# A hand-ordered attention, mixture and softplus-MLP kernel on one core: the first load of w_in moved behind the last expert matrices, and the order of everything after it written anew

## The chip, the cores and the metric

The kernel runs on one NeuronCore of a Trainium2 chip; the other seven cores are idle. The metric is device time in microseconds (us) of one execution. Five engines work side by side, each through its own instructions in program order: TensorE (PE in the profile; its weight loads are the row PEld), VectorE (DVE), ScalarE (ACT), GpSimd (POOL) and SyncE (SP), which here only issues DMA transfers. An engine that meets an instruction whose inputs are not there waits, and everything behind it on that engine waits too.

## What is computed

Three layers follow one another. The change lies behind the first.

```
x = block attention of q, k, v                        # 1536 tokens x 512
# a soft mixture of 8 experts with 4 slots each
logits = x @ phi
slot_input = softmax over tokens(logits).T @ x        # 32 x 512
for e in range(8):
    slot_out[e] = maximum(slot_input[e] @ w1[e], 0) @ w2[e]
x = softmax over slots(logits) @ slot_out             # 1536 x 512
# a softplus MLP
h = x @ w_in                                          # 512 x 2048
out = (maximum(h, 0) + log1p(exp(-abs(h)))) @ w_out   # 2048 x 512
```

## The kernel before

Everything is written as small named tasks. The string ORDER_A lists the tasks of the attention, ORDER_B those of the experts and the MLP; `run` (L188) issues them in the order of the list, and so the list alone sets the order of instructions on every engine. An engine's own order is the list with the other engines' tasks struck out. The change is a new ORDER_B; ORDER_A and all functions stay.

**Experts.** The 32 slots are one small matrix, so the time goes into loading 8 x 4 MB of weights. All transfers go through SP's one queue, 1 MB each: `w2 e h` is half h of the second matrix of expert e, `wi c h` a piece of w_in (tile wi_raw, L239), `wo b h` a piece of w_out (tile wo_raw, L249). On PE, `hu` makes the hidden rows of two experts (L751), `ht` turns them (L762), `dn e h` multiplies a half of an expert's second matrix and adds it to one sum in PSUM (so_ps, L773, four products of 512 columns), `yl n` does the last half of expert 7 in two pieces of 256 columns (L784). One source matmul of these stands as two in the trace.

**From the experts to the MLP.** `so` copies the sum out of PSUM on ACT, `ya n` adds the pieces of `yl` on DVE (L788), `yt n` turns the result on PE (L794), and `ye n` puts it into soT: the 32 slot outputs, transposed. The MLP never forms the 1536 x 512 mixture. It multiplies soT with w_in first (2048 columns in 8 parts p), as `swc 0` (L865) for part 0 and `swa p` (L850), `swb p`, `swc p` (L862) for the others; `swd p` and `swe p` put a rounded copy and its rest into cs ("SW").

**Unpacking.** w_in and w_out arrive as 64-bit numbers and are turned into 32-bit ones by hand, part by part: `wia p` or `woa p` on ACT (L680), then `wib p 0..2` or `wob p 0..2` on DVE (L686, L688, L691). `wh p` on ACT and `wl p` on DVE split a part of w_out into a high and a low half (tile whl).

**The MLP.** Half R = 0 or 1 of the tokens and column block J make step n = 16 R + J. `ha n` makes h on PE (f_ps, L881; the two banks exist once), `hx n` is the softplus on ACT (L889, tile e), `hh n` its rounded high half on ACT (gh), `hl n` the rest on DVE (gl, L732). Then 18 products of 512 columns add to six sums (acc, L907): `m n p h` are three of them, with p = 0 and 1 reading gh and p = 2 reading gl; p = 1 reads the low half of w_out, and in the first and last step of a half `m n t` does the three products of one sum. At the end of a half, `leave R t` copies a sum out (ACT or DVE) and `out R t` sends it. `swa p` and `swc p` write into spare columns of the f_ps tile of a step n, so they wait until `hx n` has read it.

```
def sw_a(p):
    ...
    o = parts["a", p] = f[2 * p - 2][:, 0, 384:512]
...
def hid(n):
    ...
    f[n] = ps_f.tile([128, 2, 512], F32, tag="f", name="f_ps")
```

The order around the change, in the list: `w2 6 1, hu 2 1, hu 3 0, wi 0 0, w2 7 0, w2 7 1`, and later `dn 5 1, yl 0, dn 6 0, dn 6 1, woa 0, dn 7 0, wob 0 0, wob 0 1, yl 1, so`.

Of the kernel before, what the change touches and what calls it, by code (L numbers as in the profile page):

```python
# [23 lines left out]
wo 1 1, wi 2 1, ya 0, wo 2 0, ct 2, ya 1, yt 0, cc 1, wob 0 2, ye 0:ACT, cc 2, yt 1, wib 1 0, wh 0, ye 1:DVE, swc 0,
wib 1 1, wia 2, wl 0:DVE, swd 0:ACT, woa 1, swe 0, wib 1 2, ha 0, fp, hx 0 0, hh 0 0, swa 1, hx 0 1, wib 2 0, wi 3 0,
wo 2 1, wi 3 1, hh 0 1, hl 0 0, m 0 0, swb 1:ACT, wia 3, hl 0 1, m 0 1, wib 2 1, ha 1, m 0 2, hx 1, wib 2 2, m 0 3,
hh 1, wob 1 0, m 0 4, woa 2, hl 1, m 0 5, swc 1, wob 1 1, m 1 0 0, swd 1:ACT, wia 4, swe 1, m 1 0 1, wob 1 2, ha 2,
m 1 1 1, hx 2, wib 3 0, wo 3 0, wo 3 1, m 1 2 1, wh 1, wib 3 1, m 1 1 0, hh 2, m 1 2 0, wl 1:DVE, m 2 0 0, hl 2,
m 2 1 0, woa 3, swa 2, wib 3 2, wia 5, m 2 2 0, swb 2:ACT, wob 2 0, ha 3, wob 2 1, m 2 0 1, hx 3, m 2 1 1, hh 3,
wob 2 2, m 2 2 1, swc 2, hl 3, wh 2, m 3 0 1, swd 2:DVE, wia 6, m 3 1 1, wl 2:DVE, m 3 2 1, swe 2, woa 4, m 3 0 0,  # L30
wib 4 0, ha 4, wib 4 1, m 3 1 0, hx 4, m 3 2 0, hh 4, wib 4 2, swa 3, hl 4, m 4 0 1, swb 3:ACT, wia 7, wob 3 0, ha 5,
m 4 1 1, hx 5, wob 3 1, m 4 2 1, hh 5, m 4 0 0, wob 3 2, m 4 1 0, hl 5, wh 3, m 4 2 0, m 5 0 0, wib 5 0, wl 3:DVE,
m 5 1 0, m 5 2 0, wib 5 1, woa 5, swc 3, m 5 0 1, swd 3:ACT, wib 5 2, m 5 1 1, swe 3, m 5 2 1, wob 4 0, ha 6,
wob 4 1, hx 6, swa 4, hh 6, wob 4 2, m 6 0 1, swb 4:ACT, hl 6, wh 4, m 6 1 1, ha 7, wib 6 0, m 6 0 0, hx 7, wl 4:DVE,
m 6 1 0, hh 7, m 6 2 0, wib 6 1, woa 6, m 6 2 1, hl 7, swc 4, m 7 0 1, swd 4:ACT, wib 6 2, m 7 1 1, swe 4, m 7 2 1,
wob 5 0, ha 8, wob 5 1, m 7 0 0, hx 8, m 7 1 0, hh 8, wob 5 2, m 7 2 0, m 8 0 0, hl 8, wh 5, m 8 1 0, wib 7 0,
m 8 2 0, wl 5:DVE, m 8 0 1, m 8 1 1, wib 7 1, woa 7, m 8 2 1, wib 7 2, swa 5, swb 5:ACT, wob 6 0, ha 9, wob 6 1,
hx 9, swc 5, hh 9, wob 6 2, m 9 0 1, swd 5:ACT, hl 9, m 9 0 0, wh 6, m 9 1 1, swe 5, wl 6:DVE, ha 10, m 9 1 0, hx 10,
m 9 2 0, wob 7 0, hh 10, wob 7 1, m 9 2 1, m 10 0 0, hl 10, m 10 1 0, wob 7 2, m 10 0 1, m 10 2 0, wh 7, swa 6,
m 10 1 1, wl 7:DVE, swb 6:ACT, ha 11, m 10 2 1, hx 11, swc 6, hh 11, swd 6:DVE, m 11 0 0, hl 11, m 11 1 0, swe 6,  # L40
m 11 2 0, ha 12, m 11 0 1, hx 12, m 11 1 1, hh 12, m 11 2 1, hl 12, m 12 0 1, m 12 0 0, m 12 1 0, m 12 2 0, m 12 1 1,
swa 7, m 12 2 1, swb 7:ACT, ha 13, hx 13, swc 7, hh 13, swd 7:DVE, m 13 0 1, hl 13, m 13 0 0, swe 7, m 13 1 0,
m 13 2 0, ha 14, m 13 1 1, hx 14, m 13 2 1, hh 14, ha 15, hl 14, m 14 0 0, hx 15, m 14 1 0, hh 15, m 14 2 0, hl 15,
m 14 0 1, m 14 1 1, m 14 2 1, m 15 4, m 15 0, ha 16, leave 0 0:ACT, m 15 3, hx 16, out 0 0, m 15 1, hh 16, m 15 5,
leave 0 1:ACT, hl 16, ha 17, out 0 1, m 15 2, hx 17, m 16 0, hh 17, leave 0 2:DVE, m 16 1, leave 0 3:ACT,
leave 0 4:DVE, out 0 2, leave 0 5:ACT, m 16 2, hl 17, out 0 3, out 0 4, out 0 5, m 16 3, m 16 4, m 16 5, ha 18,
m 17 0 1, hx 18, m 17 1 1, hh 18, m 17 2 1, hl 18, m 17 0 0, m 17 1 0, m 17 2 0, ha 19, m 18 0 0, hx 19, m 18 1 0,
hh 19, m 18 2 0, hl 19, m 19 0 0, m 19 1 0, m 18 0 1, m 18 1 1, m 18 2 1, m 19 0 1, m 19 1 1, ha 20, m 19 2 0, hx 20,
m 19 2 1, hh 20, ha 21, hl 20, m 20 0 0, hx 21, m 20 1 0, hh 21, m 20 0 1, hl 21, m 20 1 1, m 20 2 1, m 20 2 0,
m 21 0 0, m 21 0 1, m 21 1 1, m 21 2 1, ha 22, m 21 1 0, hx 22, m 21 2 0, hh 22, ha 23, hl 22, m 22 0 0, hx 23,  # L50
m 22 1 0, hh 23, m 22 2 0, hl 23, m 22 0 1, m 22 1 1, m 22 2 1, m 23 0 0, m 23 0 1, m 23 1 1, m 23 2 1, ha 24,
m 23 1 0, hx 24, m 23 2 0, hh 24, ha 25, hl 24, m 24 0 1, hx 25, m 24 0 0, hh 25, m 24 1 0, hl 25, m 24 2 0,
m 24 1 1, m 24 2 1, ha 26, m 25 0 0, hx 26, m 25 1 0, hh 26, m 25 2 0, hl 26, m 25 0 1, m 25 1 1, m 25 2 1, m 26 0 0,
m 26 1 0, ha 27, m 26 0 1, hx 27, m 26 1 1, hh 27, m 26 2 1, hl 27, m 26 2 0, ha 28, m 27 0 1, hx 28, m 27 1 1,
hh 28, m 27 2 1, hl 28, m 27 0 0, m 27 1 0, m 27 2 0, m 28 0 1, ha 29, m 28 0 0, hx 29, m 28 1 0, hh 29, m 28 2 0,
hl 29, m 28 1 1, m 28 2 1, m 29 0 1, ha 30, m 29 0 0, hx 30, m 29 1 0, hh 30, m 29 2 0, hl 30, m 29 1 1, m 29 2 1,
ha 31, m 30 0 1, hx 31, m 30 1 1, hh 31, m 30 2 1, hl 31, m 30 0 0, m 30 1 0, m 30 2 0, m 31 4, m 31 1, m 31 3,
m 31 0, m 31 5, leave 1 0:ACT, leave 1 1:DVE, out 1 1, m 31 2, out 1 0, leave 1 2:ACT, leave 1 3:DVE, leave 1 4:DVE,
# [917 lines left out]
```

## Time and profile before

| | |
|---|---|
| median of 3 runs | 317.62 us (316.42 to 318.15) |
| profiled execution | 317.56 us, its span 315.3 us, mean granted TensorE clock 0.977 |
| PE busy | 288.4 us (91% of the span) |
| DVE busy | 160.0 us (51%) |
| ACT busy | 131.1 us (42%) |
| DMA | 66.87 MB, mean 212 GB/s |
| chain that ended last, by engine | PE 61%, DVE 15%, DMA 12%, ACT 6% |
| largest line of that chain | PE acc L907, 36% |

The span runs from the first to the last instruction; 2.26 us of the execution lie around it. PE's 91% is an average over stages. The chain of waits goes back from the last instruction and names at each step what released it; its shares tell which engine the end waited for. A granted clock of 1.0 is TensorE's 2.4 GHz, 0.5 its 1.2 GHz.

### The profile page before, as it was taken

What the parts mean: (1) busy time and instruction counts of PE and PEld (TensorE: products, weight loads), DVE (VectorE), ACT (ScalarE), POOL (GpSimd) and SP (SyncE); (2) the same over time, 40 slices, a digit from 0 to 9 for tenths busy, and PEclk for the clock granted to TensorE, in tenths of its full rate; (3) what the DMA queues carried; (4) which work ended last, traced back from release to release, by engine and by line L of the source; (5) the groups of instructions that cost most, each with busy time, mean ns of one, the idle gap of its engine ahead of it and who ended that gap; (6) DMA issues with size and microseconds to landing.
All of it is one profiled execution on the core that took longest, in us unless ns stands there. A gap on an engine that the chain in (4) does not pass through costs nothing.

```text
span 315.3 us, 5651 instructions
## 1 busy us (share of the span) xinstructions
PE 288.4 (91%) x2385; PEld 196.6 (62%) x2385; DVE 160.0 (51%) x243; ACT 131.1 (42%) x197; POOL 33.5 (11%) x78
## 2 busy tenths in 40 slices
...
GB/s 237 408 421 405 420 404 418 419 418 382 273 397 70 409 424 409 403 395 400 393 401 168 0 0 3 0 0 2 0 33 166 2 0 0 0 2 0 0 0 200
DMA packets 17464, 66.87 MB, mean 212 GB/s; under 512 B 1952, under 2 KB 2080, under 8 KB 13344
## 3 DMA queue, kind: packets, MB, share of 16 engines
...
q14 instruction: 6, 0.05, 0.0%
...
## 4 chain that ended last, share of the span: by engine, by line
PE 61%; DVE 15%; DMA 12%; ACT 6%; issue 3%; SPq 1%; POOL 0%; DVEq 0%; ACTq 0%
PE acc L907 36%; DMA s<-in_moe_w 9%; PE f_ps L881 3%; PE av L365 3%; DMA s<-in_v 3%; PE tpa L349 2%; PE vs_ps L282 2%; PE sc L327 2%; DVE wf L688 2%; PE h_ps L751 2%; PE tpx L387 2%; PE so_ps L773 2%; DVE AB L339 1%; DVE m L332 1%; DVE wf L691 1%
## 5 line engine op out<-in xcount | busy, mean ns | idle before, releaser
L907 PE MATMUL acc<-whl,gh 128*128 128x512 f32 x384 | 106.6, 405 | 1.6 <-ACT gh L180 1.4
L907 PEld LDWEIGHTS acc<-whl,gh 128*128 128x128 f32 x384 | 71.5, 190 | 19.8 <-ACT gh L180 4.2
L732 DVE TENSOR_TENSOR gl<-e,gh 128x768 fp32r<-128x768 f32 (+1 forms) x33 | 30.7, 931 | 66.3 <-ACT gh L180 46.5
L907 PE MATMUL acc<-whl,gl 128*128 128x512 f32 x192 | 57.2, 396 | 0.0
L889 ACT ACTIVATE e<-f_ps 128x768 f32<-128x768 f32 (+1 forms) x33 | 26.2, 792 | 59.6 <-PE f_ps L881 58.9
L907 PEld LDWEIGHTS acc<-whl,gl 128*128 128x128 f32 x192 | 35.8, 188 | 9.1 <-issue 0.4
L180 ACT ACTIVATE gh<-e 128x768 fp32r<-128x768 f32 (+1 forms) x33 | 27.3, 826 | 1.1
L344 ACT ACTIVATE AB<-AB 128x480 f32<-128x480 f32 x24 | 13.2, 598 | 17.6 <-DVE AB L339 17.4
L881 PE MATMUL f_ps<-cs 128*128 128x384 f32 x64 | 17.0, 347 | 2.2 <-DVE cs L732 1.8
L332 DVE TENSOR_REDUCE m<-sc 128x8 f32<-128x960 f32 x12 | 13.8, 1154 | 8.8 <-PE sc L327 8.7
L349 PE MATMUL tpa<-ident,AB 128*120 128x128 f32 x96 | 14.4, 284 | 1.8 <-ACT AB L344 0.6
L881 PEld LDWEIGHTS f_ps<-cs 128*128 128x128 f32 x64 | 11.7, 190 | 6.5 <-DVE cs L732 2.8
L751 PE MATMUL h_ps<-s,siT 128*32 128x512 f32 x128 | 15.6, 648 | 0.1
L365 PE MATMUL av<-s,AB 120*64 120x65 f32 x384 | 14.0, 225 | 1.7 <-ACT AB L180 1.1
L365 PEld LDWEIGHTS av<-s,AB 120*64 120x64 f32 x384 | 12.3, 137 | 4.5 <-POOL s L258 2.2
L773 PE MATMUL so_ps<-s,hT 128*32 128x512 f32 x104 | 14.6, 697 | 0.0
L339 DVE TENSOR_TENSOR AB<-sc,m 128x960 f32<-128x960 f32 x12 | 13.9, 1155 | 1.4 <-PE tpa L349 0.7
L180 ACT ACTIVATE AB<-tpa 120x512 f32<-120x512 f32 x23 | 13.1, 593 | 3.1 <-PE tpa L349 3.0
L618 PE MATMUL wm<-warm_x 128*128 128x480 bf16 x43 | 13.1, 449 | 1.2 <-DVE warm_x L599 1.2
...
L349 PEld LDWEIGHTS tpa<-ident,AB 128*120 128x120 f32 x96 | 10.0, 137 | 6.2 <-ACT AB L344 1.8
L680 ACT ACTIVATE wo<-wo_raw 128x1024 f32<-128x1024 f32 x8 | 9.2, 1147 | 10.8 <-DMA wo_raw<-in_moe_w_out 6.3
(130 smaller groups left out, 311.1 us busy)
## 6 DMA issues: line engine op xcount, KB each, us to landing
...
```

What stands on the lines that cost most here:

```text
L180: nc.scalar.activation(out=o, in_=i, func=ACTF.Copy)
L332: nc.vector.tensor_reduce(out=m.rearrange("p (e u) -> p e u", e=2), in_=sc_t[i][:, :, 0:480].rearrange("p e (u j) -> p e u j", u=4), axis= ...
L339: nc.vector.tensor_tensor(out=A_t[i], in0=sc_t[i][:, :, 0:480].rearrange("p e (u j) -> p e u j", u=4), in1=m_t[i].rearrange("p (e u) -> p ...
L344: nc.scalar.activation(out=A_t[i][:, e], in_=A_t[i][:, e], func=ACTF.Exp, scale=0.125)
L349: nc.tensor.transpose(tp[0:120, u], A_t[i][:, e, u, :], ident)
L365: mm(out=av_t[i][64 * w:64 * w + 64, e, 65 * u:65 * u + 65], lhsT=AT_t[i][0:120, e, c:c + 64], rhs=v_t[g][0:120, 4 * n + 2 * t + w, 2 * a ...
L732: (nc.vector if eng == "DVE" else nc.gpsimd).tensor_tensor(out=o, in0=i, in1=h.bitcast(F32), op=ALU.subtract)
L751: mm(out=h_ps[E][32 * j:32 * j + 32], lhsT=siT[:, kk], rhs=w1_t[2 * E + j // 2, n][:, kk % 2, 512 * (j % 2):512 * (j % 2) + 512], start=(k ...
L773: mm(out=so_ps[32 * m:32 * m + 32, 0], lhsT=hT[e // 4][:, e % 4, h, m], rhs=w2_t[e, h, m], start=(e == 0 and h == 0), stop=(e == 7 and h = ...
L881: mm(out=f[n][:, h, 0:384], lhsT=cs_t["SW"][:, J], rhs=cs_t["cS"][:, s0:s0 + 384], **one)
L889: nc.scalar.activation(out=e_[n][:, half(hs)], in_=f[n][:, half(hs), 0:384], func=ACTF.Softplus)
L907: mm(out=acc[R, t], lhsT=g, rhs=(wh, wl, wh)[p][J], start=(J == 0 and p == 0), stop=(J == 15 and p == 2))
```

## The change

The string ORDER_B is replaced by another order of the same tasks. Seven tasks change their engine: `swd 2` and `swd 6` go from DVE to ACT, and five of the twelve copies `leave` at the ends of the halves are dealt out anew. Of the diff two lines say what leads it:

```
-w2 5 1, w2 6 0, hu 2 0, w2 6 1, hu 2 1, hu 3 0, wi 0 0, w2 7 0, w2 7 1, hu 3 1, ht 0, wo 0 0, wi 0 1, wi 1 0, wo 0 1,
+w2 5 1, w2 6 0, hu 2 0, w2 6 1, w2 7 0, hu 2 1, w2 7 1, hu 3 0, wi 0 0, hu 3 1, ht 0, wo 0 0, wi 0 1, wi 1 0, wo 0 1,
...
+wia 0, dn 5 1, wib 0 0, dn 6 0, wib 0 1, dn 6 1, woa 0, wib 0 2, dn 7 0, wob 0 0, wob 0 1, yl 0, so, yl 1, wia 1,
```

**Place 1, SP and PE at the last experts.** SP's queue before, from the last w2 loads on:

```order
L231 DMA s<-in_moe_w 128x2048 x8
L239 DMA wi_raw<-in_moe_w_in 128x4x512
L231 DMA s<-in_moe_w 128x2048 x2
L249 DMA wo_raw<-in_moe_w_out 128x2x1024
L239 DMA wi_raw<-in_moe_w_in 128x4x512 x2
```

and of the change:

```order
L231 DMA s<-in_moe_w 128x2048 x10
L239 DMA wi_raw<-in_moe_w_in 128x4x512
L249 DMA wo_raw<-in_moe_w_out 128x2x1024
L239 DMA wi_raw<-in_moe_w_in 128x4x512 x2
```

The first piece of w_in stood ahead of both halves of expert 7 and now stands behind them; from wo_raw on the queue is as it was. PE before, from the experts 4 to 7 (hT_1407) to the first part of w_in:

```order
L773 MATMUL so_ps<-s,hT_1407 32x512 x16
L784 MATMUL so_ps<-s,hT_1407 32x256 x4
L773 MATMUL so_ps<-s,hT_1407 32x512 x12
L784 MATMUL so_ps<-s,hT_1407 32x256 x4
L670 MATMUL ct_ps<-ident,cw 128x128 x8
L794 MATMUL sT_ps<-e_99,so 128x128 x4
L865 MATMUL sw_ps<-wf,soT 128x128 x8
```

and of the change:

```order
L773 MATMUL so_ps<-s,hT_1407 32x512 x28
L784 MATMUL so_ps<-s,hT_1407 32x256 x8
L670 MATMUL ct_ps<-ident,cw 128x128 x4
L794 MATMUL sT_ps<-e_99,so 128x128 x4
L865 MATMUL sw_ps<-wf,soT 128x128 x8
```

`yl 0` stood ahead of the last three `dn` (x12) and now stands with `yl 1` behind them; one `ct` went forward. On DVE the order from the first `wib` to `swe 0` is the same in both: `wib 0 0..2`, `wob 0 0`, `wob 0 1`, then `ya`; on ACT `so` stands behind `woa 0` in both.

**Place 2, PE in the steps 3 to 5 (f_ps L881 is `ha`, L850 `swa 3`, L862 `swc 3`).** Of the change:

```order
L907 MATMUL acc<-whl,gl 128x512 x3
L881 MATMUL f_ps<-cs 128x384 x2
L850 MATMUL f_ps<-wf,soT 32x128 x8
L907 MATMUL acc<-whl,gh 128x512 x3
L881 MATMUL f_ps<-cs 128x384 x2
L907 MATMUL acc<-whl,gh 128x512 x3
```

`ha 4` and `swa 3` had six products of step 3 between them and now stand side by side. The same pair side by side was there before at `ha 6`, `swa 4`, and is there now at `ha 4`, `ha 6` and `ha 8`; the pair `ha`, `swc` was side by side before at `ha 9` and `ha 13`.

**Place 3, PE between the two halves of the tokens (the sums of step 15 in threes: two of gh, one of gl).** Before:

```order
L907 MATMUL acc<-whl,gl 128x512
L881 MATMUL f_ps<-cs 128x384 x2
L907 MATMUL acc<-whl,gh 128x512 x2
L907 MATMUL acc<-whl,gl 128x512
L907 MATMUL acc<-whl,gh 128x512 x2
L907 MATMUL acc<-whl,gl 128x512
L907 MATMUL acc<-whl,gh 128x512 x2
L907 MATMUL acc<-whl,gl 128x512
L881 MATMUL f_ps<-cs 128x384 x2
L907 MATMUL acc<-whl,gh 128x512 x2
```

and of the change:

```order
L907 MATMUL acc<-whl,gh 128x512 x2
L907 MATMUL acc<-whl,gl 128x512
L907 MATMUL acc<-whl,gh 128x512 x2
L907 MATMUL acc<-whl,gl 128x512
L881 MATMUL f_ps<-cs 128x384 x4
L907 MATMUL acc<-whl,gh 128x512 x2
L907 MATMUL acc<-whl,gl 128x512
```

`ha 16` stood after two of the six sums of step 15 and `ha 17` after five; now both stand behind all six, next to each other (x4), and ahead of the first sum of step 16. On ACT the copies `leave 0 0`, `leave 0 2` and `leave 0 3` stand ahead of `hx 16`. At the very end the last sum is in both orders `m 31 2`; behind its copy on ACT, `leave 1 2`, the list now has one more copy on ACT, `leave 1 5`, which was on DVE.

## Rows read from the trace of the kernel before

**Rows 1.** Chain that ended last: start, us, what (the last expert loads, the products behind)

```profile
110.83 20.19 DMA s<-in_moe_w
132.23 5.00 PE so_ps L773 x24
```

**Rows 2.** Timeline 120 to 138 us: start, us, engine, line, tile, count [idle before <-releaser]

```profile
121.95 3.64 PE L773 MATMUL so_ps<-s,hT 128*32 128x512 f32 x32
131.15 1.08 PE L784 MATMUL so_ps<-s,hT 128*32 128x256 f32 x8 [5.56 <-DMA s<-in_moe_w]
...
126.25 1.12 ACT L680 ACTIVATE wf<-wi_raw 128x1024 f32<-128x1024 f32 x1 [6.92 <-DMA wi_raw<-in_moe_w_in]
133.62 1.14 ACT L680 ACTIVATE wo<-wo_raw 128x1024 f32<-128x1024 f32 x1 [6.26 <-DMA wo_raw<-in_moe_w_out]
137.32 0.60 ACT L180 ACTIVATE so<-so_ps 128x512 f32<-128x512 f32 x1 [2.55 <-PE so_ps L773]
...
129.39 1.22 DVE L691 SCALAR_TENSOR_TENSOR wf<-wi_raw,wf 128x1024 int32<-128x1024 int32 x1
...
137.95 0.42 DVE L788 TENSOR_TENSOR so<-so_ps,so 128x256 f32<-128x256 f32 x1 [1.19 <-ACT so L180]
```

**Rows 3.** Timeline 138 to 146 us, the way into the MLP

```profile
138.49 0.65 PE L794 MATMUL sT_ps<-e,so 128*128 128x128 f32 x4
...
140.34 2.35 PE L865 MATMUL sw_ps<-wf,soT 128*128 128x128 f32 x16
...
143.33 0.43 DVE L732 TENSOR_TENSOR cs<-sw_ps,cs 64x256 fp32r<-64x256 f32 x1
...
145.74 0.73 PE L907 MATMUL acc<-whl,gh 128*128 128x512 f32 x2
```

**Rows 4.** Stages: from:to, us, busy PE, PEld, DVE, ACT, POOL, granted clock, DMA

```profile
131.10:137.60 6.50, 6.45 (x41) 1.99 (x41) 1.92 (x2) 1.43 (x2) 0.00 (x0) 0.55 1.04 390
...
160.00:178.00 18.00, 17.77 (x93) 13.27 (x92) 17.64 (x20) 11.95 (x14) 0.00 (x0) 1.00 0.51 197
```

**Rows 5.** Timeline 178 to 223 us: steps 6, 9 and 13 on PE, step 6 on ACT

```profile
178.01 0.62 PE L881 MATMUL f_ps<-cs 128*128 128x384 f32 x2 [0.25 <-DVE cs L732]
178.66 0.81 ACT L889 ACTIVATE e<-f_ps 128x768 f32<-128x768 f32 x1 [2.09 <-PE f_ps L881]
179.51 0.85 ACT L180 ACTIVATE gh<-e 128x768 fp32r<-128x768 f32 x1
...
179.53 0.64 PE L850 MATMUL f_ps<-wf,soT 128*32 128x128 f32 x16 [0.90 <-ACT e L889]
...
180.41 0.50 PE L907 MATMUL acc<-whl,gh 128*128 128x512 f32 x1 [0.23 <-ACT gh L180]
...
198.00 3.91 PE L907 MATMUL acc<-whl,gh 128*128 128x512 f32 x9 [0.38 <-ACT gh L180]
...
222.69 2.37 PE L907 MATMUL acc<-whl,gh 128*128 128x512 f32 x9 [0.38 <-ACT gh L180]
```

**Rows 6.** A stretch of one us at step 9, columns as rows 4

```profile
199.00:200.00 1.00, 1.00 (x3) 0.76 (x3) 0.97 (x2) 0.87 (x1) 0.00 (x0) 0.50 0.00 0
```

**Rows 7.** Chain that ended last: one `ha`, `swc`, `swa`, and 36 products

```profile
182.07 0.35 PE f_ps L881 x2
...
185.23 0.42 PE f_ps L862 x4
...
207.17 0.57 PE f_ps L850 x16
...
301.94 8.42 PE acc L907 x36
```

**Rows 8.** The page's costliest groups: busy us, mean ns of one | idle before

```profile
L732 DVE TENSOR_TENSOR gl<-e,gh 128x768 fp32r<-128x768 f32 (+1 forms) x33 | 30.7, 931 | 66.3 <-ACT gh L180 46.5
```

**Rows 9.** Timeline, the last product and the last copy

```profile
309.94 0.40 PE L907 MATMUL acc<-whl,gl 128*128 128x512 f32 x1
...
310.38 0.60 ACT L180 ACTIVATE ot<-acc 128x512 f32<-128x512 f32 x1 [0.80 <-PE acc L907]
```

More of the change, by code (lines that the diff above doesn't have):

```diff
@@ L24 @@
[L24 to L58, printed above, removed]
@@ L59 @@
-out 1 3, leave 1 5:DVE, out 1 4, out 1 5, out 1 2
+hu 0 0, c 0, w2 3 0, hu 0 1, w2 3 1, w2 4 0, hu 1 0, hr 0, w2 4 1, c 1, c 2, w2 5 0, hu 1 1, c 3, c 5, c 4, c 6,
+w2 5 1, w2 6 0, hu 2 0, w2 6 1, w2 7 0, hu 2 1, w2 7 1, hu 3 0, wi 0 0, hu 3 1, ht 0, wo 0 0, wi 0 1, wi 1 0, wo 0 1,
+wi 1 1, ct 0, hr 2, hc 0 0, dn 0 0, hc 0 1, cc 0, dn 0 1, dn 1 0, dn 1 1, ht 2, hr 1, hc 2 1, hc 2 0, ht 1, ct 1,
+hc 1 1, hr 3, hc 1 0, dn 2 0, cc 1, dn 2 1, ht 3, dn 3 0, hc 3 1, hc 3 0, dn 3 1, dn 4 0, wo 1 0, dn 4 1, dn 5 0,
@@ new lines @@
+wia 0, dn 5 1, wib 0 0, dn 6 0, wib 0 1, dn 6 1, woa 0, wib 0 2, dn 7 0, wob 0 0, wob 0 1, yl 0, so, yl 1, wia 1,
+ya 0, ct 2, wi 2 0, ya 1, wo 1 1, wi 2 1, wo 2 0, yt 0, wob 0 2, cc 2, ye 0:ACT, yt 1, wib 1 0, wh 0, ye 1:DVE,
+swc 0, wib 1 1, wia 2, wl 0:DVE, swd 0:ACT, woa 1, swe 0, wib 1 2, ha 0, fp, hx 0 0, hh 0 0, swa 1, hx 0 1, wib 2 0,
+wi 3 0, wo 2 1, wi 3 1, hh 0 1, hl 0 0, m 0 0, wia 3, hl 0 1, m 0 1, wib 2 1, swb 1:ACT, m 0 2, wib 2 2, ha 1, m 0 3,
+woa 2, wob 1 0, m 0 4, hx 1, wob 1 1, m 0 5, hh 1, swc 1, hl 1, m 1 0 0, wia 4, wob 1 2, m 1 1 0, swd 1:ACT, m 1 0 1,
@@ new lines @@
+swe 1, wh 1, wo 3 0, wo 3 1, m 1 1 1, wib 3 0, m 1 2 1, wib 3 1, ha 2, m 1 2 0, wl 1:DVE, hx 2, swa 2, hh 2, wib 3 2,
+m 2 0 1, woa 3, m 2 0 0, wob 2 0, swb 2:ACT, wia 5, hl 2, ha 3, m 2 1 1, hx 3, wob 2 1, m 2 2 1, hh 3, m 2 1 0, hl 3,
+m 2 2 0, wob 2 2, m 3 0 0, wia 6, m 3 0 1, wib 4 0, wh 2, swc 2, wib 4 1, m 3 1 1, swd 2:ACT, m 3 2 1, wl 2:DVE,
+m 3 1 0, swe 2, woa 4, m 3 2 0, wib 4 2, ha 4, hx 4, wob 3 0, swa 3, hh 4, wob 3 1, m 4 0 1, swb 3:ACT, wia 7, hl 4,
+ha 5, m 4 1 1, hx 5, wob 3 2, m 4 2 1, hh 5, wib 5 0, swc 3, wh 3, m 4 0 0, hl 5, swd 3:ACT, m 4 1 0, swe 3,
```

31 lines of the change are left out of this document (27 added, 4 removed).

## The prediction

> **What bounds the kernel now.** I read the chain of waits first, because it shows what the end waited for. Up to 131 us it is the loading of the expert matrices: the last link of it is one DMA piece of 20.19 us, and then 24 products on PE [rows 1]. The timeline of that place [rows 2] shows why these products are slow and late. PE was done with expert 5 at 125.59 (121.95 + 3.64). The next instruction in its queue was `yl 0`, which needs the very last load; it waited 5.56 us, and with it the products of expert 6 and of the first half of 7, whose data lay there. Then the 24 products took 5.00 us, 0.21 each, where 32 of the same kind had taken 3.64, 0.114 each: the granted clock from 131.1 to 137.6 has a mean of 0.55 [rows 4], that is mostly 1.2 GHz after an idle stretch, and 2.4 GHz before it. `so` began on ACT at 137.32, and DVE waited 1.19 us for it.
>
> From `ya` at 137.95 on, DVE and ACT share the chain with PE until about 200 us. In the stage from 160 to 178 us PE is busy 17.77 us of 18 and DVE 17.64 [rows 4]: neither has room, and a delay of one is a delay of both. From 223 us to the end PE alone counts: 36 products take 8.42 us [rows 7] back to back. So the question is how much idle PE time goes ahead of 146 us, and how much the new order puts in or takes out behind it. The sum is made against the profiled execution, 317.56 us (span 315.3 and 2.26 around it), which is the median of the runs within 0.1 us.
>
> **A. The experts' end, -0.45 us.** The loads land one behind another: ACT got w_in's first piece at 126.25, PE the last expert half at 131.15 two loads later, ACT w_out's first at 133.62 [rows 2], so about 2.45 us each. In the new queue the two expert halves land at about 126.2 and 128.7 and w_in's piece at 131.15; w_out's stays. PE then does its 24 products as the data come, at 2.4 GHz, and both `yl` by about 130: the 5.56 us wait and the half-speed products are gone from there. But little of it reaches `ya`. `so` stands on ACT behind `woa 0`, whose load lands at 133.62, so it begins at 134.8. And `ya` stands on DVE behind five field operations. The first three cannot begin before 131.15 + 1.12 = 132.3, and take 3.24 us (126.25 + 1.12 to 129.39 + 1.22 [rows 2]): 135.5. The two of w_out take the same less the third field, 3.24 - 1.22 = 2.0: 137.5. `ya` was at 137.95. Bounds: nothing gained, and -1.2, DVE's whole wait.
>
> **B. The clock on the way into the MLP, +2.0.** What is late next is PE itself. It now idles from about 130 to 137.5, longer than the 5.56 us after which it ran at 1.2 GHz, and so begins the critical part there: `yt`, `swc 0`, `ha 0`. Before, the slow stretch fell on the 24 products and was over at 137. The two groups of `yt` take 0.65 each at most and the `swc 0` 2.35 with a wait of about 0.2 to 0.7 in it [rows 3]; at the ratio 0.21/0.114 = 1.85 they take some 2.8 us more. Some 0.8 of that fits into waits that are there now. `swe 0`, at 143.33 before, and the first product of `m 0 0`, at 145.74, come 2.0 later by this term. Bounds: 0, the clock being back by then; and +3.8, if the first products of step 0 are slow too (one slow stretch cost 1.8, see C).
>
> **C. Steps 0 to 12, -1.7.** From the first product to step 13 the trace has 222.69 - 145.74 = 76.95 us. The work in it is 13 x 18 products at 0.234 (8.42/36), 54.7; 13 `ha` at 0.35, 4.6; 6 `swa` at 0.57, 3.4; 7 `swc` at 0.42, 2.9 [rows 7]: 65.6. So 11.3 are lost. A round trip is seen at step 6 [rows 5]: `swa 4` starts 1.52 after `ha 6`, the next product 2.40 after it. A pair `ha`, `swa` side by side thus costs 1.52 - 0.35 = 1.17, then 2.40 - 1.52 - 0.57 = 0.31: 1.5. A pair `ha`, `swc` costs 1.6. Before, the order forces 5.7: the pair at step 6, pairs with `swc` at 9 (with a further 0.4 for the copy ahead of it) and 13, and 0.6 where three products stand between, at 11. At step 9 the clock also fell: 0.50 at 199 us [rows 6], nine products in 3.91 instead of 2.1 [rows 5], 1.8 lost. The new order forces 6.2: pairs at 4, 6 and 8, 4.5, and 1.7 at 2 and 13, where three products stand between. Waits of this length did not drop the clock at step 6, so I take the 1.8 as saved: 6.2 - 5.7 - 1.8 = -1.3. `swd 2` leaves the full DVE, about -0.4, the size of `swe` [rows 3]. Bounds: -3.6, if half of what is left of the 11.3 (3.8, waits for DVE and changes of tile) goes as well; and +0.1, if one of the new pairs drops the clock.
>
> **D. Between the halves, +2.3.** Before, `ha 16` lay under the sums of step 15 and cost nothing. Now it is behind all of them. Count from the end of the last one, 0: the copy `leave 0 3` starts on ACT 0.2 later (310.38 against 309.94 + 0.234 [rows 9]) and ends at 0.8; `hx 16` runs to 1.6, `hh 16` to 2.45 [rows 5], `hl 16` on DVE 0.93 more, about 3.45 with the handing over [rows 8]. PE does `ha 16` to 0.35, waits for `hx 16`, does `ha 17` from 1.65 to 2.0, starts `m 16 0` at 2.5, and its third product, which needs gl, waits from 2.97 to 3.5. Lost: 1.3 + 0.5 + 0.5. Bounds: 1.6, if ACT is early; and 4.1 if the clock falls there as at step 9.
>
> **E. Later steps, +1.5.** The new list has `ha 21, m 20 2 1, hx 21, hh 21, ha 22, hx 22, m 21 0 1`: three products and `ha 22` under a round trip of 1.52 and 2.40, so 0.47 and 0.52 are lost. `m 31 0` needs gl of step 31, 2.40 + 0.93 = 3.33 after `ha 31`; PE is there at 0.35 + 3 x 0.70 + 0.47 = 2.9: 0.5. **F. The end, +0.6.** One more copy on ACT, 0.60 [rows 9], stands behind the last one, and its transfer goes out last.
>
> **Sum:** -0.45 + 2.0 - 1.7 + 2.3 + 1.5 + 0.6 = +4.25, from 317.56 to **321.8 us**. What is moved past SP's queue costs nothing: the DMA share is 1.04 at 131 to 137 us [rows 4], so the transfers wait for each other and not for SP.
>
> **Rivals.** *The clock is never low behind the experts* (B is 0): for it speaks that `yt` could fall into a stretch that the chip still grants; against it the idle time, longer than one that did lower it. 317.56 + 2.25 = 319.8, and within 0.5% (1.6 us, about what a measurement of this kernel can tell from no change) if C goes a little further. *The clock falls again*, at a pair or between the halves: +1.8 to +3.6, 323.6 to 325.4; for it speaks step 9, against it step 6. *The other side: PE no longer waits for DVE between 146 and 223 us.* In place of 11.3 only the forced 6.2 would be lost, C is -5.1; with the clock up at `yt` that makes -0.45 - 5.1 + 4.4 = -1.15, 316.4, or a little below. It decides at `ha 4` and `ha 10`: if `swe 2` and `swe 5` are done before PE gets there, this holds. Against it: DVE is busy 17.64 of 18 us and does the same fields as before. [...]
>
> **Chances.** Forecast 0.52; clock never low 0.15, of which 0.09 within 0.5%; clock falling again 0.15; other side 0.13, of which 0.08 faster by over 0.5%; landings unchanged 0.05. So faster 0.08, same 0.09 + 0.05 = 0.14, slower 0.78. The range leaves out the other side, part of the clock rival and the worst of the bounds: 318.3 to 325.5.
>
> **What would show it.** In the profile of the change PE should idle from about 130 to 137.5, the clock be 0.5 behind it, `ya` start near 137.5, `m 0 0` near 147.3, PE wait about 1.2 between `ha` and `swa` at steps 4, 6 and 8, and 2.3 in all at the change of halves. If `m 0 0` starts before 146, B is wrong; if PE is dense between the halves, D; if step 13 starts 5 us earlier counted from `m 0 0`, the other side holds.

## The result and the profile after

The changed kernel takes 320.88 us, median of 16 executions (317.6 to 324.69), beside 316.47 of the kernel before (16 executions, 314.09 to 318.35): ratio 1.0116, 95% interval 1.0086 to 1.0145, so 3.7 us slower (2.7 to 4.6). The ratio leaves out executions that lie over 1.5% above the fastest of their kernel, three of the 16 of the change, so it is below the 1.0139 of the two medians. The profiled execution took 321.95 us, its span 320.2, mean granted clock 0.963 (before 0.977); it is 4.39 longer than the profiled one of before.

The loads landed as their new order says: both halves of expert 7 (`yl` at 128.51), then w_in's first piece (its copy at 130.74), then w_out's (133.18). Timeline of the change, 124 to 152 us, PE, then ACT and DVE (start, us, engine, line, tile, count [idle before <-releaser]):

```profile
123.79 4.90 PE L773 MATMUL so_ps<-s,hT 128*32 128x512 f32 x44
128.51 1.05 PE L784 MATMUL so_ps<-s,hT 128*32 128x256 f32 x16
...
137.36 1.22 PE L794 MATMUL sT_ps<-e,so 128*128 128x128 f32 x4 [7.22 <-DVE so L788]
139.05 1.22 PE L794 MATMUL sT_ps<-e,so 128*128 128x128 f32 x4 [0.47 <-ACT soT L180]
140.06 3.48 PE L865 MATMUL sw_ps<-wf,soT 128*128 128x128 f32 x16
...
146.40 1.09 PE L907 MATMUL acc<-whl,gh 128*128 128x512 f32 x2
...
150.15 0.52 PE L881 MATMUL f_ps<-cs 128*128 128x384 f32 x2
```

```profile
130.74 1.12 ACT L680 ACTIVATE wf<-wi_raw 128x1024 f32<-128x1024 f32 x1 [11.72 <-DMA wi_raw<-in_moe_w_in]
133.18 1.14 ACT L680 ACTIVATE wo<-wo_raw 128x1024 f32<-128x1024 f32 x1 [1.32 <-DMA wo_raw<-in_moe_w_out]
134.22 0.59 ACT L180 ACTIVATE so<-so_ps 128x512 f32<-128x512 f32 x1
...
136.89 0.75 DVE L788 TENSOR_TENSOR so<-so_ps,so 128x256 f32<-128x256 f32 x2
```

The 5.56 us wait ahead of `yl 0` [rows 2] is gone, the expert products run at 0.11 each and end at 129.6. But `ya` begins at 136.89, behind five field operations, and PE idles 7.22 us until `yt`. There each group takes 1.22 instead of 0.65 and 0.71, and `swc 0` 3.48 instead of 2.35 [rows 3]. The clock in stages (from:to, us, busy PE, PEld, DVE, ACT, POOL, granted clock, DMA share, GB/s):

```profile
134.00:143.00 9.00, 5.17 (x22) 4.85 (x23) 7.96 (x10) 4.88 (x7) 0.00 (x0) 0.50 1.04 395
143.00:146.00 3.00, 1.34 (x14) 0.85 (x17) 2.04 (x4) 2.18 (x4) 0.00 (x0) 0.97 1.04 399
147.00:149.00 2.00, 2.00 (x6) 1.52 (x5) 1.39 (x2) 1.97 (x5) 0.00 (x0) 0.50 1.03 406
160.00:178.00 18.00, 16.87 (x89) 12.67 (x89) 16.65 (x18) 13.09 (x18) 0.00 (x0) 1.00 0.47 182
239.00:242.00 3.00, 3.00 (x8) 2.32 (x9) 0.96 (x1) 0.33 (x1) 0.00 (x0) 0.50 0.07 25
```

Between the experts' end and the last product TensorE's granted clock falls to 0.50 three times: on the way into the MLP, in the 7.22 us of idle time and behind it; in step 0, after a stretch in which PE was busy 1.34 of 3 us; and behind the change of halves. That one, on PE's timeline:

```profile
235.38 0.52 PE L881 MATMUL f_ps<-cs 128*128 128x384 f32 x2
236.93 0.62 PE L881 MATMUL f_ps<-cs 128*128 128x384 f32 x2 [1.03 <-ACT e L889]
237.81 0.73 PE L907 MATMUL acc<-whl,gh 128*128 128x512 f32 x2 [0.26 <-ACT gh L180]
238.80 0.79 PE L907 MATMUL acc<-whl,gl 128*128 128x512 f32 x1 [0.26 <-DVE gl L732]
239.39 1.06 PE L907 MATMUL acc<-whl,gh 128*128 128x512 f32 x2
```

`ha 16`, `ha 17`, the first products and gl each wait, as the prediction had counted; then two products take 1.06, where they took 0.62 to 0.63 elsewhere.

**Where the 4.9 us of span went.** I count from `woa 0`, the start of w_out's first copy, because the time at which the loads land turned out to differ by up to 5.1 us between executions (`woa 0` at 131.00 to 136.14 in the table below). Landing: -0.44 (133.62 to 133.18). `woa 0` to `yt`: 4.87 to 4.18, -0.69 (A). `yt` to the first product of step 0: 7.25 to 9.04, +1.79 (B). From there to the first sum of step 15: 86.46 to 84.78, -1.68 (C). From there to the last product: 77.74 to 82.18, +4.44 (D, E and the clock). Last product to the end of the span: 5.36 to 6.84, +1.48 (F). Together 4.90; the part of an execution that lies around the span was 0.5 shorter, which leaves the 4.39.

### The profile page after: what moved, and what is told of

Same layout as the page of the kernel before. It is cut to its first block, busy times and chain, and to the rows that moved or that the text cites. A ratio compares the mean times of both kernels' runs of the same rounds, so it can differ in the third digit from the quotient of the medians.

```text
span 320.2 us, 5651 instructions
## 1 busy us (share of the span) xinstructions
PE 288.8 (90%) x2385; PEld 199.8 (62%) x2385; DVE 158.3 (49%) x240; ACT 131.7 (41%) x200; POOL 33.4 (10%) x78
## 5 line engine op out<-in xcount | busy, mean ns | idle before, releaser
L907 PE MATMUL acc<-whl,gl 128*128 128x512 f32 x192 | 58.6, 403 | 0.5 <-DVE gl L732 0.5
L907 PEld LDWEIGHTS acc<-whl,gl 128*128 128x128 f32 x192 | 36.7, 192 | 9.6 <-DVE gl L732 1.3
L881 PE MATMUL f_ps<-cs 128*128 128x384 f32 x64 | 17.0, 346 | 2.2 <-ACT e L889 1.2
L881 PEld LDWEIGHTS f_ps<-cs 128*128 128x128 f32 x64 | 11.7, 189 | 6.1 <-ACT e L889 2.0
L680 ACT ACTIVATE wf<-wi_raw 128x1024 f32<-128x1024 f32 x8 | 9.2, 1147 | 12.8 <-DMA wi_raw<-in_moe_w_in 12.8
L327 PE MATMUL sc<-s 64*64 64x120 f32 x384 | 12.7, 266 | 0.2 <-POOL s L258 0.2
```

Of the source, the lines that this page charges most:

```text
L881: mm(out=f[n][:, h, 0:384], lhsT=cs_t["SW"][:, J], rhs=cs_t["cS"][:, s0:s0 + 384], **one)
L907: mm(out=acc[R, t], lhsT=g, rhs=(wh, wl, wh)[p][J], start=(J == 0 and p == 0), stop=(J == 15 and p == 2))
```

## The experiments

The list was cut in three at places where both orders have issued the same tasks: the head (to `hl 0 0`), the middle (`m 0 0` to step 14) and the tail (from the sums of step 15). All numbers in the table are from the profiled executions: start of `woa 0`, then `yt 0` and the first product of step 0 counted from it, then the stages from that product to the first sum of step 15 and on to the last product; the last column has the ratio to the kernel before, measured beside it. A star marks a stretch at a granted clock of 0.50 in a stage behind `yt 0`.

| kernel | woa 0 | yt 0 | m 0 0 | to step 15 | to the last product | ratio (95%) |
|---|---|---|---|---|---|---|
| before | 133.62 | 4.87 | 12.12 | 86.46* | 77.74 | |
| change | 133.18 | 4.18 | 13.22* | 84.78* | 82.18* | 1.0116 (1.0086 to 1.0145) |
| head_only | 135.61 | 4.16 | 13.28* | 85.46* | 77.75 | 1.0053 (1.0016 to 1.009) |
| mid_only | 132.00 | 4.49 | 11.74 | 83.93 | 77.75 | 0.9922 (0.9887 to 0.9957) |
| tail_only | 132.96 | 4.24 | 11.49 | 86.45* | 80.66 | 1.0076 (1.0042 to 1.011) |
| warm | 134.60 | 10.36 | 17.39 | 83.93 | 80.66 | 1.0191 (1.0146 to 1.0236) |
| halves_undone | 132.54 | 4.21 | 13.05* | 84.52* | 78.32 | 1.0020 (0.9978 to 1.0061) |
| old_head | 135.67 | 4.26 | 11.51 | 83.92 | 80.66 | 1.0038 (1.0001 to 1.0075) |
| warm_bank | 134.55 | 4.23 | 11.36 | 83.93 | 80.66 | 1.0027 (0.9986 to 1.0068) |
| warm_old_tail | 136.14 | 4.23 | 11.36 | 83.92 | 77.75 | 0.9869 (0.9792 to 0.9946), of 2 executions of 6 |
| warm_old_tail_2 | 135.64 | 4.23 | 11.51 | 84.57* | 77.75 | 0.9964 (0.9928 to 1.0) |
| load_moved | 131.00 | 4.23 | 12.45* | 84.72* | 77.74 | 0.9951 (0.9913 to 0.9989) |
| yl_moved | 133.64 | 3.49 | 12.74* | 84.70* | 77.74 | 1.0012 (0.998 to 1.0044) |
| mid_warm | 133.50 | 3.57 | 10.70 | 84.71* | 77.74 | 0.9884 (0.9848 to 0.9921) |

**One part of the change at a time.** The theory was that the waits between and behind the halves and the low clock ahead of the MLP make the loss; the rival, that the moved load does.

head_only, against the change: from `m 0 0` on the order of before.

```
 hh 0 1, hl 0 0,
-m 0 0, wia 3, hl 0 1, m 0 1, wib 2 1, swb 1:ACT,
+m 0 0, swb 1:ACT, wia 3, hl 0 1, m 0 1,
...
```

> The new order up to the first product of step 0 (the moved load, both yl behind the last dn, the longer idle time of PE), the old order from there to the end. Theory (the loss is in part the clock on the way into the MLP): PE idles about 7.2 us instead of 5.6 + 1.2, the granted clock is 0.5 from about 133 to 143 us, the first product starts near 146.4 instead of 145.7, and a second slow stretch may follow in step 0 as in the profile of the change (1.6 more): 0.7 to 2.3 slower than before, ratio 1.002 to 1.007. Rival (the moved load alone makes most of the loss): +3 to +5, ratio 1.010 or more. Rival (what the head loses is made up behind it by waits that are there anyway): 0, ratio 1.000.

mid_only, against before: the order of the change from `m 0 0` to the end of step 14.

```
 hl 0 0,
-m 0 0, swb 1:ACT, wia 3, hl 0 1, m 0 1,
+m 0 0, wia 3, hl 0 1, m 0 1, wib 2 1, swb 1:ACT,
...
 m 15 4, m 15 0, ha 16, leave 0 0:ACT,
```

> Old order up to the first product of step 0, new order of the steps 0 to 14, old order from the sums of step 15 on. Theory: the new order of the middle is the one part that gains. In the profile of the change the stage from the first product to step 13 took 75.27 us against 76.95, although it held a slow stretch of the clock worth 1.6; without that stretch it would be about 3.3 shorter. So 1.7 to 3.3 faster than before, ratio 0.990 to 0.995. Rival (the old middle lost its 1.8 at step 9 by chance of one execution, and the rest is even): 0, ratio 1.000.

tail_only, against before: the order of the change from the sums of step 15 to the end.

```
-m 15 4, m 15 0, ha 16, leave 0 0:ACT, m 15 3, hx 16,
+m 15 5, m 15 4, m 15 1, m 15 0, m 15 2, leave 0 0:ACT,
...
```

> Old order up to the end of step 14, new order from the sums of step 15 to the end (ha 16 and ha 17 behind all of step 15, ha 21 and ha 22 three products apart, one more copy on ACT at the end). Theory: this part holds nearly the whole loss: 2.3 between the halves, 1.6 more if the clock falls there, 1.5 in the later steps, 0.6 to 1.5 at the end: 4.4 to 6 slower than before, ratio 1.014 to 1.019, and the gap between the last sum of step 15 and m 16 0 reads 2.4 us as in the change. Rival (the change's loss comes from the head, and the tail only shows the slow clock that the head set off): below 2.3, ratio under 1.007, with a granted clock of 1.00 between the halves.

The head costs 1.7 us (0.0053), the middle gains 2.5, the tail costs 2.4. The head's stages are those of the change: 13.28 and a stretch at a granted clock of 0.50 in step 0 (150 to 152 us). The middle takes 83.93 when the clock stays up (1.00 from 137 to 300 us), 2.5 less than before (1.7 to 3.3 were expected). The tail shows the waits of the change at a granted clock of 1.00, and its stage is 2.91 longer. Timeline and stage of tail_only between the halves:

```profile
235.09 0.51 PE L881 MATMUL f_ps<-cs 128*128 128x384 f32 x2
236.64 0.62 PE L881 MATMUL f_ps<-cs 128*128 128x384 f32 x2 [1.04 <-ACT e L889]
237.52 0.73 PE L907 MATMUL acc<-whl,gh 128*128 128x512 f32 x2 [0.26 <-ACT gh L180]
238.51 0.50 PE L907 MATMUL acc<-whl,gl 128*128 128x512 f32 x1 [0.26 <-DVE gl L732]
238.85 0.63 PE L907 MATMUL acc<-whl,gh 128*128 128x512 f32 x2
```

```profile
239.00:242.00 3.00, 3.00 (x15) 2.41 (x14) 0.96 (x1) 0.04 (x1) 0.00 (x0) 1.00 0.00 0
```

The waits are the same to 0.01, the clock is 1.00 where it was 0.50 in the change. The tail's loss of 2.4 missed its expected 4.4 to 6 and is near the rival's 2.3: in the profile the clock did not fall, as the rival had it, and steps 16 to 31 lost less than predicted. That the tail only shows a slow clock from elsewhere is wrong all the same, since the waits stand there at full clock. The three ratios add to 1.0051, the change has 1.0116; each part is uncertain by 0.0035. Stage by stage each part has in its own stage what the change has there; what is left over is the stretch at 0.50 between the halves (1.52), the one in step 0 (0.85) and the end.

**The change of halves undone.** Against the change:

```
-m 15 5, m 15 4, m 15 1, m 15 0, m 15 2, leave 0 0:ACT, leave 0 1:DVE, out 0 1, m 15 3,
-out 0 0, leave 0 2:ACT, ha 16, out 0 2, leave 0 3:ACT, leave 0 4:DVE, leave 0 5:DVE,
+m 15 4, m 15 0, ha 16, leave 0 0:ACT, m 15 3, hx 16, out 0 0, m 15 1, hh 16, m 15 5,
+leave 0 1:ACT, hl 16, ha 17, out 0 1, m 15 2, hx 17, m 16 0, hh 17, leave 0 2:DVE, m 16 1,
...
```

> The change with one stretch put back: the sums of step 15 and the first three of step 16 in the old order, so that ha 16 lies behind two of the sums of step 15 and ha 17 behind five. Theory (2.3 of the loss is the wait between the halves, and 1.5 more in executions in which the clock falls behind it): PE is dense from the first sum of step 15 to step 17, the stage takes 9.1 as before instead of 11.45 to 13.0, and the time falls by 2.3 to 3.9, from a ratio to the kernel before of 1.0116 to 1.0043 to 0.999. Rival (the change of halves only waits for what is late anyway, and the loss turns up at ha 18 or at the end): under 1 us gained, ratio 1.009 or more.

The ratio falls from 1.0116 to 1.0020, 3.0 us (uncertain by some 1.6), inside the expected 2.3 to 3.9. The stage from step 15 takes 78.32, against 80.66 with the waits and no fall of the clock: the waits are worth 2.34. What stands above the 77.74 of before, 0.57, is term E.

**The old head again.** Against the change, the order of before up to `hl 0 0`; of it the first edits:

```
-w2 5 1, w2 6 0, hu 2 0, w2 6 1, w2 7 0, hu 2 1, w2 7 1, hu 3 0, wi 0 0, hu 3 1, ht 0,
+w2 5 1, w2 6 0, hu 2 0, w2 6 1, hu 2 1, hu 3 0, wi 0 0, w2 7 0, w2 7 1, hu 3 1, ht 0,
...
```

> Old order up to the first product of step 0 (w_in's piece ahead of the last expert matrices again, yl 0 ahead of the last three dn), the change's order behind it. Theory A (the parts add): the middle alone gave 0.9922 and the tail alone 1.0076, so 0.9998, that is 3.7 faster than the change, which is more than the 1.7 that the new head cost by itself. Theory B (the slow clock of the new head sets off further falls, and without it none comes in step 0 or between the halves): the same 1.000, with a granted clock of 1.00 in step 0 and between the halves. Rival (what falls between the halves comes from the wait there, whatever the head was): the clock falls there again and the ratio is 1.003 to 1.006.

Expected 1.000, measured 1.0038 (1.0001 to 1.0075). In its profile the clock is 1.00 in step 0 and between the halves, as both theories had it; with the change it fell at both. One execution of each can't show that the new head causes the fall between the halves: that stays open.

**PE kept busy in its idle time.** First into so's own tile:

```
-wia 1, ya 0, ct 2, wi 2 0,
+wia 1, ya 0, ct 2, warm 32, wi 2 0,
```

> The change with 32 products of zeros (bfloat16, 480 columns, into the unused bank of so_ps) put on PE between the last yl and the first yt, where PE idled 7.2 us; the result does not use them. Theory (the idle time lowers the clock): the products take about 0.2 each, end near 136.7, the granted clock stays at 1.00 there, yt takes 0.65 instead of 1.22 a group, swc 0 2.35 instead of 3.5, the first product of step 0 starts near 144.9 instead of 146.4, and no slow stretch follows in step 0: 1.5 to 3.1 faster than the change, so a ratio to the kernel before of 1.002 to 1.007. Rival (the clock falls there whatever PE does in that time): no gain, 1.0116 as the change, or more, since products at 1.2 GHz would end later than 136.9 and delay yt by some us.

This missed. The products wrote into the PSUM tile that `so` reads, so they waited for `so` (row `<-ACT so`) and stood in the way of `yt`:

```profile
131.25 0.66 PE L670 MATMUL ct_ps<-ident,cw 128*128 128x128 f32 x4
136.28 8.85 PE L618 MATMUL so_ps<-warm_x 128*128 128x480 bf16 x32 [4.37 <-ACT so L180]
144.96 0.61 PE L794 MATMUL sT_ps<-e,so 128*128 128x128 f32 x4
```

They began after 4.37 us of idle time, and 32 of them took 8.85, 0.28 each on average (granted clock 0.50 from 134 to 140 us). With a bank of their own:

```
-wia 1, ya 0, ct 2, wi 2 0,
+wia 1, ya 0, ct 2, wb, warm 30, wi 2 0,
...
+    task(("wb",), lambda: wm.append(bank("wm_ps")))
```

> The run called warm failed of its purpose: its products waited for so on ACT, since they wrote into so's own PSUM tile. Now 30 products of zeros go into a PSUM bank of their own behind the last ct; the rest is the change, and the result does not use them. Theory (PE's idle time lowers the clock): they run from about 130.5 to 136.7 at 0.2 each, the granted clock is 1.00 from there to step 0, and the first product of step 0 starts 11.4 to 11.5 behind the start of woa 0 instead of 13.2; with the second fall in step 0 (1.6) gone as well 1.8 to 3.4 faster than the change, ratio 1.001 to 1.006. Rival (the clock is not what the head costs): the first product 13.2 behind woa 0 as in the change, ratio 1.0116.

```profile
131.50 6.24 PE L618 MATMUL wm_ps<-warm_x 128*128 128x480 bf16 x30
138.78 0.71 PE L794 MATMUL sT_ps<-e,so 128*128 128x128 f32 x4 [1.05 <-DVE so L788]
139.97 0.71 PE L794 MATMUL sT_ps<-e,so 128*128 128x128 f32 x4 [0.47 <-ACT soT L180]
140.52 2.35 PE L867 MATMUL sw_ps<-wf,soT 128*128 128x128 f32 x16
```

```profile
126.00:300.00 174.00, 163.84 (x850) 121.94 (x843) 92.89 (x103) 83.55 (x108) 0.00 (x0) 1.00 0.28 109
```

The only edit is work whose result is thrown away, and the kernel is 2.8 us faster than the change (1.0116 to 1.0027). `yt` stands 4.2 behind `woa 0` in both; `yt` and `swc 0` take 0.71, 0.71 and 2.35 again; the first product comes at 11.36 instead of 13.22, and the granted clock is 1.00 up to 300 us, between the halves too. So what the new head costs behind `yt` is the clock. In these two profiles it is 0.50 behind 7.22 us of idle time (the change, 134 to 143 us) and 1.00 behind the 30 products.

**With the old tail.** warm_bank with the order of before from the sums of step 15 on:

```
-m 15 5, m 15 4, m 15 1, m 15 0, m 15 2, leave 0 0:ACT,
+m 15 4, m 15 0, ha 16, leave 0 0:ACT, m 15 3, hx 16,
...
```

> The same 30 products, the change's order up to the end of step 14, the old order from the sums of step 15 on: the new head without its slow clock, the middle that gained, the old tail. Theory: the middle gives the 0.9922 that it gave alone; the head, with the clock up, is 0 to 0.7 shorter than the old one (yt 4.2 behind woa 0 instead of 4.2 to 4.9): 0.990 to 0.9925, some 6.5 faster than the change and 2.5 to 3.2 faster than the kernel before. Rival (the middle's gain hangs on the old head): 0.996 to 1.000.

> The kernel of warm_old_tail once more, since its executions lay between 311.55 and 316.91 and its profiled one had woa 0 at 136.1, against 132.0 in mid_only. Theory (where the loads land is chance of the execution and not of the order; by stages counted from woa 0 the kernel is 0.4 shorter than mid_only): median 313.5 to 314.5, ratio 0.989 to 0.992. Rival (the products of zeros delay something outside the stages, or the clock falls elsewhere for them): median near 316, ratio 0.995 to 0.999.

The two runs of this kernel gave 0.9869 and 0.9964. The first ratio counts only the two fastest of six executions (311.55 and 314.07); the median of the six is 316.28, that of the twelve in the second run 316.23. So the expected 0.989 to 0.9925 was missed, the numbers are those of the rivals, and the kernel is not shown to be faster than mid_only (314.15). By stages the kernel is as short as the theory says (11.36 and 83.92, or 84.57 with a stretch at 0.50 in step 0), but in both profiles `woa 0` began late, at 136.14 and 135.64. With w_in's piece in its new place `woa 0` began at 131.00 to 136.14 (8 profiles, mean 134.2), in its old place at 132.00 to 135.67 (6 profiles, mean 133.6). Whether the new queue lands later on the average is not to be told from these; what makes this kernel slower than its stages say stays open.

**Two edits of the head apart**, against mid_only (the head's other edits, such as the order of `hr`, `ht` and `hc`, were not taken apart). load_moved:

```
-w2 6 1, hu 2 1, hu 3 0, wi 0 0, w2 7 0, w2 7 1,
+w2 6 1, hu 2 1, hu 3 0, w2 7 0, w2 7 1, wi 0 0,
```

> The rest is mid_only (old head, new middle, old tail), in which one thing of the new head is put in: w_in's first piece behind the two halves of expert 7 in SP's queue; yl 0 stays ahead of the last three dn. Theory (the clock costs, the load does not): the last half lands some 5 before woa 0 instead of 2.5, so PE idles about 3 instead of 5.6 to 6.1 ahead of yl 0 and then again until yt, which starts 4.2 behind the start of woa 0. If the slow stretch falls on the 24 products and is over at yt, the first product of step 0 comes 11.4 behind woa 0: 0.1 to 0.7 less than in mid_only, ratio 0.990 to 0.992. Rival (the load itself makes the new head slow, since fields and so are late): first product 12.5 or more behind woa 0, ratio 0.996 to 0.999.

yl_moved:

```
-dn 5 0, dn 5 1, yl 0, dn 6 0, dn 6 1, woa 0, dn 7 0, wob 0 0, wob 0 1, yl 1,
+dn 5 0, dn 5 1, dn 6 0, dn 6 1, woa 0, dn 7 0, wob 0 0, wob 0 1, yl 0, yl 1,
```

> The rest is mid_only, in which the other thing of the new head is put in: yl 0 behind the last dn, ahead of yl 1; the loads stay. Theory (what costs is that PE has nothing left to do from the last load to yt): PE works off the products of experts 6 and 7 as they land, then idles some 4 to 5 until yt; if the granted clock is 0.50 at yt as in the new head, the first product of step 0 comes 12.5 to 13.3 behind the start of woa 0 instead of 11.5 to 12.1, and a slow stretch follows in step 0: 1 to 2.5 slower than mid_only, ratio 0.995 to 1.000. Rival (the moved load costs): as mid_only or better, ratio 0.990 to 0.992, first product 11.4 behind woa 0.

`yl_moved` shows it: 0.009 slower than mid_only (2.9 us, a little more than expected), 9.25 us from `yt` to the first product of step 0 (9.04 in the change, 7.25 before), and the two groups of `yt` at half clock (0.50 from 138 to 142 us) though the load stands where it was:

```profile
131.18 1.07 PE L784 MATMUL so_ps<-s,hT 128*32 128x256 f32 x16 [1.52 <-DMA s<-in_moe_w]
...
137.13 1.23 PE L794 MATMUL sT_ps<-e,so 128*128 128x128 f32 x4 [3.85 <-DVE so L788]
138.83 1.22 PE L794 MATMUL sT_ps<-e,so 128*128 128x128 f32 x4 [0.47 <-ACT soT L180]
```

The moved load alone is undecided: 0.9951 lies between the two expectations, its interval overlaps that of mid_only, and in its profile the clock fell twice ahead of step 0 (0.57 from 126 to 130 us, 1.00 from 131 to 136, 0.67 from 138 to 141), after 3.03 us of idle time ahead of `yl 0` and after 3.04 ahead of `yt`, so the second fall hit `yt 1` and `swc 0`. What the load does by itself is seen at `yt`: 3.49 and 3.57 behind `woa 0` where w_in's piece is early and PE not late (yl_moved, mid_warm), 4.16 to 4.23 where it is moved (but for warm, whose products stood in the way). DVE's three fields of w_in then stand ahead of `ya`: 0.7 us given away.

**The old head kept busy.** In mid_only:

```
-dn 5 0, dn 5 1, yl 0, dn 6 0,
+dn 5 0, dn 5 1, wb, warm 26, yl 0, dn 6 0,
...
+    task(("wb",), lambda: wm.append(bank("wm_ps")))
```

> mid_only with 26 products of zeros into a PSUM bank of their own ahead of yl 0, in the 5.6 to 6.1 in which PE waits there for the last load. Theory: the clock is 1.00 when the last half lands, the 24 products take 2.7 instead of 4.6 to 5.2, so starts right behind woa 0, yt 4.2 behind the start of woa 0 (4.5 in mid_only), and if the clock holds until yt the first product of step 0 comes 11.4 behind woa 0: 0.1 to 0.7 less than mid_only, ratio 0.990 to 0.992. Rival (it only moves the fall): PE idles again some 3 ahead of yt, the granted clock is 0.50 there, and the first product comes 12.5 or more behind woa 0: ratio 0.995 or more.

```profile
125.90 5.44 PE L618 MATMUL wm_ps<-warm_x 128*128 128x480 bf16 x26
131.27 0.64 PE L784 MATMUL so_ps<-s,hT 128*32 128x256 f32 x8
131.73 2.76 PE L773 MATMUL so_ps<-s,hT 128*32 128x512 f32 x24
```

The 24 products take 2.76 instead of 5.00 [rows 1], the first product of step 0 comes 10.70 behind `woa 0`, the earliest of all; a stretch at 0.50 in step 0 (145 to 147 us) gives 0.8 of that back. Its ratio is 0.9884 (0.9848 to 0.9921; median 313.36, six executions), the expectation 0.990 to 0.992. With mid_only it is the fastest version; which of the two is better the intervals don't say. The theory's 11.4 was passed by 0.7 because `ya` no longer waits for `so`: `yt` comes at 3.57, not at 4.2.

## Why the prediction came out as it did

The time was forecast at 321.8 and is 320.88; the sum was +4.25, the profiled executions differ by 4.39, and the ratio says 3.7. The mechanisms of A, B and D are as they were given. The sum itself is close in part by luck: without the fall of the clock between the halves (1.52) and the late end of that one execution, the terms as measured add to about +2.5 (-0.69, +1.79, -1.68, +2.34, +0.57, +0.15).

- **A, -0.45:** -0.69. The five field operations ahead of `ya` were right. The figure was 0.24 low: `ya` came 3.71 behind `woa 0`, where I had 3.88 (137.5 - 133.62), and in the old order `yt` began 0.54 behind `ya`, in the new one 0.47.
- **B, +2.0:** +1.79, by the mechanism that was given, and in warm_bank the first product comes 1.86 earlier. The bound for "the first products of step 0 slow too" came true as well; in the stage to step 15 it costs 0.6 to 0.85 (84.52 and 84.78 against 83.93), less than the 1.8 that I had put on one slow stretch. Against mid_only, product by product, the change is 1.24 behind at the 24th product and 0.80 at the 48th: the difference is won back around `ha 3`, where mid_only loses some time itself. What PE waits for there the trace does not name.
- **C, -1.7:** measured -1.68, near the forecast by luck: two gains and a loss of another size than forecast. With the clock up the new middle takes 83.93, 2.5 less than before. About 1.7 of that is the stretch at a low clock that the old middle had in both profiles in which the clock was up on its way in (0.50 at step 9, and a mean of 0.86 between 178 and 190 us in tail_only). It is hardly the chance of one execution: the mean clock of mid_only's executions has a median of 0.980, that of the kernel before beside it 0.976, and one stretch is worth 0.005 (some 3 us at 0.50 in a span of 315). The remaining 0.7 to 0.9 (85.46 in head_only against 84.52 to 84.78, each with a stretch in step 0) is a gain by the order, where I had counted pairs and `swd 2` and got +0.1. The stretch in step 0 (0.85) takes a third of the 2.5 back. The pairs cost what I said (0.90 to 1.02 of wait ahead of each `swa`). Where the order saves, the waits of PE that the trace names in this stage show. In before they are 5.33 us, in mid_only 4.57: the waits at `ha` for DVE's part of SW (0.41 and 0.25, the latter in [rows 5]) and for ACT's copy (0.40) are gone, those for ACT around the pairs went from 4.27 to 4.57. Between head_only and the change, the pair with a stretch in step 0, the sums are 4.94 and 4.54, so there about half of the gain has no name. Before, `ha 2` and `ha 9`, and mid_only, `ha 4` and its `swa`:

```profile
153.02 0.62 PE L881 MATMUL f_ps<-cs 128*128 128x384 f32 x2 [0.41 <-DVE cs L732]
195.61 0.62 PE L881 MATMUL f_ps<-cs 128*128 128x384 f32 x2 [0.40 <-ACT swg L180]
```

```profile
165.03 0.54 PE L881 MATMUL f_ps<-cs 128*128 128x384 f32 x2
166.47 0.64 PE L850 MATMUL f_ps<-wf,soT 128*32 128x128 f32 x16 [0.90 <-ACT e L889]
```

  Which of the moved tasks makes DVE early enough, `swd 2` on ACT or the rest of the order, no run takes apart.
- **D, +2.3:** 2.34 (80.66 against 78.32), at the three places that were named, and taking it out gains 3.0 in the measured time. The bound of 4.1 for a fall of the clock nearly came true in the profiled execution: 2.34 + 1.52 = 3.86. In four other profiles with the same tail it did not fall.
- **E, +1.5:** 0.57. This is the mis-sized term. The three waits stand where they were named, at `ha 22`, `m 21` and `m 31 0`:

```profile
262.74 0.62 PE L881 MATMUL f_ps<-cs 128*128 128x384 f32 x2 [0.20 <-ACT e L889]
263.62 2.37 PE L907 MATMUL acc<-whl,gh 128*128 128x512 f32 x9 [0.26 <-ACT gh L180]
...
309.06 1.20 PE L907 MATMUL acc<-whl,gl 128*128 128x512 f32 x4 [0.20 <-DVE gl L732]
```

  Start to start they cost 0.36 (1.41 from `ha 21` to `ha 22`, where 0.35 and three products make 1.05), 0.53 (0.88 instead of 0.35) and 0.36: 1.25, near the forecast; for the third wait the working gives 3.33 - 2.9 = 0.4, where it says 0.5. What the step left out is a gain. In the old order PE lost 0.18 behind three of the `ha` of this half, 0.53 to 0.54 from their start to the next product instead of 0.35; one of them in before, and one of the change:

```profile
254.98 0.51 PE L881 MATMUL f_ps<-cs 128*128 128x384 f32 x2
255.52 1.67 PE L907 MATMUL acc<-whl,gh 128*128 128x512 f32 x6
```

```profile
244.15 0.52 PE L881 MATMUL f_ps<-cs 128*128 128x384 f32 x2
244.51 1.57 PE L907 MATMUL acc<-whl,gh 128*128 128x512 f32 x6
```

  The others are at 264.39 and 273.79; behind the `ha` of the change in the later steps it is 0.35 to 0.36. The product behind each such place also comes 0.10 to 0.11 late. With that the new order loses 1.45 in this half and the old one 0.88, and the difference is the 0.57. I had read only the waits that the trace names, and no idle time stands at these rows.
- **F, +0.6:** 0.1 to 0.2. The stage from the last product to the end takes 5.54 to 5.67 in the five other profiles with the new end and 5.36 to 5.58 with the old one. The two copies on ACT take 1.08 together, not 0.60 each, so the last one ends 0.48 later, and what follows it was 0.30 shorter in tail_only (4.07 against 4.37 before). The 6.84 of the change was that execution alone; its page has one packet more in the instruction queue (19, where before and tail_only have 18), and that this is the cause is not shown.

The rivals: the clock was low behind the experts (0.50 from 134 to 143 us), so that one falls. The clock did fall again, between the halves, in the profiled execution. The other side needed C at -5.1; it is -1.7, or -2.5 with the clock up. Its sign did come: from the first product of step 0 to the first sum of step 15 the trace of the change names no wait of PE for DVE. But in before these were only 0.66 us, under a fifth of the 3.8 that I had put down to waits for DVE and changes of tile. The loads landed as issued: w_in's piece behind both expert halves, w_out's 2.44 behind it; with the queue the landings changed, so the 0.05 for unchanged ones falls.
